# Reordering the first loads of a fused attention and token-mixing kernel: two row tiles first, the key weights in single chunks, a transpose of its own for tile 3

## The chip, the cores and the metric

One core of a Trainium2 chip runs the kernel. The metric is device time in microseconds, the median of several executions. The profile is of one more execution, and its span runs from the first to the last instruction.

## What is computed

With x of 2048 rows and 512 columns, the reference mixes two branches by a gate for each row:

```python
def _A_ref(x, wqkv, wo):                 # linear attention, 32 heads of 16
    q, k, v = split(x @ wqkv)
    phi = lambda t: where(t > 0, t + 1, exp(t)) + 1e-6
    pq, pk = phi(q), phi(k)
    kv = einsum("bhsd,bhse->bhde", pk, v)
    z = einsum("bhsd->bhd", pk)
    num = einsum("bhqd,bhde->bhqe", pq, kv)
    den = einsum("bhqd,bhd->bhq", pq, z)[..., None] + 1e-6
    return (num / den) @ wo
def _B_ref(x, w1, b1, w2, b2):           # MLP over the rows, F = 1792
    h = layernorm(x)
    u = gelu(einsum("bsd,sf->bdf", h, w1) + b1)
    return transpose(einsum("bdf,fs->bds", u, w2) + b2)
g = sigmoid((x * gate_w).sum(-1, keepdims=True))
out = g * _A_ref(x, wqkv, wo) + (1 - g) * _B_ref(x, w1, b1, w2, b2)
```

All inputs and the output are bf16.

## The kernel before

The rows are cut into 16 tiles of 128. `xs` holds x with rows on partitions, `xT` holds it with columns on partitions, in four blocks of 128 columns (k = 0 to 3). Every instruction's order on its engine is written by hand; the schedule is not planned by a tool. Each engine works through its own list and waits by semaphores, and so do the two queues from which DMAs are issued here, SP's (`nc.sync`) and ACT's (`nc.scalar`).

The stages, in order:

1. *Keys and G.* For each row tile t, four matmuls of 512 columns (`k_part`, tile `kacc`, all recorded at line 110 by the helper `mm`) multiply x's blocks by `wk_sb`, the key third of wqkv. `k_phi` then makes `pk` with an exponential on ScalarE (L216) and two operations on VectorE (L217, L220). Four tiles later `g_tile` adds x-transposed times pk into four accumulators (`gacc`). `ln_step` takes a tile's layer norm statistics on VectorE (L240, L241).
2. *The first three W1 blocks, with the queries* (`uacc`, `qacc`), from 32 us on. Their weights are the first of four chunks of W1 (`w1c`).
3. *The rest of W1*, with the small products of the attention branch in between.
4. *The output*: for each row tile, `aps` (attention) and `yps` (MLP), mixed and stored.

The transposed blocks come in two ways. Tiles 0 to 2 (`HEADS = 3`) are transposed on TensorE: `transpose_part(t, k0, k1)` multiplies blocks of `xs` by an identity into a PSUM bank `pt`, and `copy_part` copies the bank into `xT`, on ScalarE (L210) or VectorE (L212). Tiles 3 to 15 are transposed by DMA straight from the input (`load_xT`, L132), on SP's queue.

The first DMAs are issued by `load_x` (L126) and `load_wk` (L129). SP gets x0, x1 and the third chunk of Wk (Wk 2); ACT gets the first two chunks in one transfer (Wk 0-1), x2 and the fourth chunk (Wk 3). A chunk or an x tile is 128 KB. The first DMA transpose is held back: VectorE copies a few elements of x0 into the place that the transpose will write (L156), so that the transpose has to wait for that copy, and the copy for x0's landing. Behind it SP issues the transpose of tiles 5 to 7, x3, x4 to x7, and then transposes and rows in groups of four, Wq, and W1's first chunk in two halves of 1024 KB.

While the first data is on its way, TensorE runs six matmuls on constants (`warm_up(6)`, tile `wps`), and ScalarE loads its table (L196). TensorE then does tile 0's four transposes, the first two K matmuls of tile 0, the transposes of tiles 1 and 2, and the remaining ten K matmuls of the three tiles, chunk by chunk; then the loop over tiles 3 to 15 begins.

Of the kernel before, what the change touches and what calls it, by code (L numbers as in the profile page):

```python
# [15 lines left out]
def kernel(  # L16
# [13 lines left out]
    nc = tc.nc  # L30
    P = nc.NUM_PARTITIONS
# [8 lines left out]
    NT = S // P  # L40
    ND = D // P
# [15 lines left out]
    w1_view = B_w1.rearrange("(t p) f -> p t f", p=P)  # L57
# [8 lines left out]
    def keep(shape, dtype, name):  # L66
        return persist.tile(shape, dtype, name=name, tag=name)

    def bank(name, dtype=FP32):
        return ps.tile([P, SC], dtype, name=name, tag="bank")  # L70

    xs = keep([P, NT, D], BF16, "xs")
    hs = keep([P, NT, D], BF16, "hs")
    xT = keep([P, ND, S], BF16, "xT")
# [34 lines left out]
    def mm(o, lhsT, rhs, start, stop, **kw):  # L109
        nc.tensor.matmul(o, lhsT=lhsT, rhs=rhs, start=start, stop=stop, **kw)  # L110
# [14 lines left out]
    def load_x(q, t0, n):  # L125
        q.dma_start(out=xs[:, t0 : t0 + n, :], in_=x_view[:, t0 : t0 + n, :])  # L126

    def load_wk(q, k, n):
        q.dma_start(out=wk_sb[:, k : k + n, :], in_=wqkv_view[:, k : k + n, D : 2 * D])  # L129

    def load_xT(t0, n):
        nc.sync.dma_start(  # L132
            out=xT[:, :, t0 * P : (t0 + n) * P], in_=X[t0 * P : (t0 + n) * P, :], transpose=True
        )

    load_x(nc.sync, 0, 1)
    load_wk(nc.scalar, 0, 2)
    load_x(nc.sync, 1, 1)
    load_x(nc.scalar, 2, 1)
    load_wk(nc.sync, 2, 1)  # L140
    load_wk(nc.scalar, 3, 1)
    nc.vector.memset(ones_f[:], 1.0)
    nc.vector.memset(mhalf[:], -0.5)
    nc.gpsimd.memset(ident[:], 0.0)
    nc.gpsimd.affine_select(
        out=ident[:], in_=ident[:], compare_op=ALU.not_equal, fill=1.0, base=0,
# [5 lines left out]
        out=maskQ[:], in_=maskH[:].rearrange("p (a m) -> p m a", m=2), op=ALU.max, axis=AX.X  # L152
    )
    nc.gpsimd.memset(brow[:], 0.0)

    nc.vector.tensor_copy(  # L156
        out=xT[:, :, 3 * P : 3 * P + 2],
        in_=xs[:, 0, 0 : 2 * ND].rearrange("p (k c) -> p k c", k=ND),
    )
    load_xT(3, 2)  # L160
    load_xT(5, 3)
    load_x(nc.sync, 3, 1)
    load_x(nc.sync, 4, 4)
    for t0, n in ((8, 4), (12, 4)):
        load_xT(t0, n)
        load_x(nc.sync, t0, n)
# [2 lines left out]
    for c, (j0, nb) in enumerate(w1_chunks):  # L169
        w = wpool.tile([P, NT, FB * P], BF16, name="w1c", tag="wc")  # L170
        w1c.append(w)
        for t0 in range(0, NT, 8) if c == 0 else (0,):
            t1 = t0 + 8 if c == 0 else NT
            nc.sync.dma_start(
                out=w[:, t0:t1, : nb * P], in_=w1_view[:, t0:t1, j0 * P : (j0 + nb) * P]
            )
        if c == 0:
            nc.sync.dma_start(out=wv_sb[:], in_=wqkv_view[:, :, 2 * D : 3 * D])
            nc.sync.dma_start(out=wo_sb[:], in_=wo_view)
# [21 lines left out]
    def transpose_part(t, k0, k1):  # L201
        pt = pts[t, k0, k1] = bank("pt")
        for k in range(k0, k1):
            mm(pt[:, k * P : (k + 1) * P], xs[:, t, k * P : (k + 1) * P], ident[:], True, True)

    def copy_part(t, k0, k1, on_act):
        src = pts.pop((t, k0, k1))[:, k0 * P : k1 * P].rearrange("p (k s) -> p k s", k=k1 - k0)
        dst = xT[:, k0:k1, t * P : (t + 1) * P]
        if on_act:
            nc.scalar.activation(out=dst, in_=src, func=ACT.Copy)  # L210
        else:
            nc.vector.tensor_copy(out=dst, in_=src)  # L212

    def phi(dst, acc):
        e = work.tile([P, SC], BF16, name="e", tag="e", bufs=6)
        nc.scalar.activation(out=e[:], in_=acc[:], func=ACT.Exp)  # L216
        nc.vector.tensor_scalar(  # L217
            out=e[:], in0=e[:], scalar1=1.0, scalar2=PHI_EPS, op0=ALU.min, op1=ALU.add
        )
        nc.vector.scalar_tensor_tensor(  # L220
            out=dst, in0=acc[:], scalar=0.0, in1=e[:], op0=ALU.max, op1=ALU.add
        )
# [3 lines left out]
    def k_part(t, ks):  # L226
        if t not in kaccs:
            kaccs[t] = bank("kacc")
        for k in ks:
            mm(  # L230
                kaccs[t][:], xT[:, k, t * P : (t + 1) * P], wk_sb[:, k, :],
                k == 0, k == ND - 1,
            )

    def k_phi(t):
        phi(pk[:, t, :], kaccs.pop(t))
# [46 lines left out]
    def ln_step(u):  # L283
        ln_stats(u)
        if u % TPC == TPC - 1:
            ln_rstd(u // TPC)

    HEADS = 3
    for k0, k1 in ((0, 1), (1, 2), (2, ND)):
        transpose_part(0, k0, k1)  # L290
        copy_part(0, k0, k1, k0 == 2)
    k_part(0, range(2))
    for k0, k1 in ((0, 1), (1, 2), (2, ND)):
        transpose_part(1, k0, k1)
    for k0, k1 in ((0, 2), (2, ND)):
        transpose_part(2, k0, k1)
    copy_part(1, 0, 1, False)
    copy_part(1, 1, 2, True)
    copy_part(2, 0, 2, False)
    copy_part(2, 2, ND, True)  # L300
    copy_part(1, 2, ND, False)
    k_part(1, range(2))
    k_part(2, range(2))
    ln_step(0)
    for t in range(HEADS):
        k_part(t, (2,))
    for t in range(HEADS):
        k_part(t, (3,))
        k_phi(t)
    ln_step(1)  # L310
    LAG = 4
    LN_LAG = 5
# [147 lines left out]
    for j in range(NB0, NF):  # L460
        c, jj = divmod(j, FB)
# [30 lines left out]
        out=gg[:], in0=gth[:], scalar1=0.5, scalar2=0.5, op0=ALU.mult, op1=ALU.add  # L492
    )
    nc.vector.tensor_scalar(
        out=c1[:], in0=gth[:], scalar1=-0.5, scalar2=0.5, op0=ALU.mult, op1=ALU.add
# [3 lines left out]
    for t in range(NT):  # L499
        c, tl = divmod(t, TPC)  # L500
        aps = bank("aps")
        for j in range(ND):
# [3 lines left out]
            out=a_sc[:], in_=aps[:], func=ACT.Identity,  # L506
            scale=gg[:, t : t + 1], bias=c2[:, t : t + 1],
        )
        for c0, W in ((0, 2 * P), (2 * P, P), (3 * P, P)) if t == NT - 1 else ((0, D),):
            cs = slice(c0, c0 + W)  # L510
            yps = bank("yps")
            for f in range(NF):
# [6 lines left out]
                out=ot[:, :W], in0=yps[:, :W], scalar=c1[:, t : t + 1], in1=a_sc[:, cs],  # L519
# [35 lines left out]
```

## Time and profile before

| What | Before |
|---|---|
| Median of 3 runs | 162.54 us (162.47 to 163.53) |
| Profiled execution, first to last instruction (the only time that its page gives) | 160.8 us |
| TensorE busy | 156.3 us (97%) |
| VectorE busy | 124.8 us (78%) |
| ScalarE busy | 72.8 us (45%) |
| GpSimd busy | 7.3 us (5%) |
| Granted TensorE clock, mean | 1.000 |
| HBM read, written | 19.01 MB, 2.10 MB |

A line of the timeline or of a group names the engine (PE is TensorE, PEld its weight loads, DVE VectorE, ACT ScalarE, POOL GpSimd, SPq SP's queue), the source line, the operation, the tile written and the tiles read, and how many instructions were merged. A bracket gives the idle time ahead and what ended it. Matmuls are pipelined and their ends are modelled, so groups of matmuls overlap in the timeline by a little; it is the distance of their starts that says how fast they go.

### The profile page before, as it was taken

How to read it: one execution, taken by the hardware profiler on the slowest of the kernel's cores; microseconds unless marked ns; L12 is line 12 of the kernel's file. 1: busy time of each engine (PE TensorE's matmuls, PEld its weight loads, DVE VectorE, ACT ScalarE, POOL GpSimd, SP SyncE). 2: the span in 40 equal slices, each digit the busy share in tenths (PEclk: the TensorE clock that was granted, in tenths of full speed). 3: DMA queues.
4: the chain of work that ended last, by engine and by line, in shares of the span. 5: the costliest groups of instructions: out<-in, count | busy, mean ns of one | idle time of the engine just before them, and what ended most of it. 6: DMA issues, size and time to landing. Idle time of an engine off the chain costs nothing.

```text
span 160.8 us, 2241 instructions
## 1 busy us (share of the span) xinstructions
PE 156.3 (97%) x826; PEld 72.6 (45%) x840; DVE 124.8 (78%) x276; ACT 72.8 (45%) x114; POOL 7.3 (5%) x17
## 2 busy tenths in 40 slices
PE   7999999999999999999999999999999999999993
PEld 2444444444444444444444444444444444444462
DVE  1599999769999998756999999676999999711122
ACT  3552476654978483059873330237433442111110
POOL 3000332002020000000000000000000000000000
PEclk9999999999999999999999999999999999999999
DMA  5999999999970007600930689501000001110001
GB/s 165 229 235 238 274 335 295 359 348 348 335 177 0 0 0 236 225 0 5 335 120 2 186 270 288 169 33 37 33 33 33 33 33 60 47 60 33 33 33 33
DMA packets 29369, 22.94 MB, mean 143 GB/s; under 512 B 7824, under 2 KB 29328, under 8 KB 29360
## 3 DMA queue, kind: packets, MB, share of 16 engines
q1 hardware_dynamic: 28400, 21.89, 46.1%
q10 hardware_dynamic: 848, 0.79, 1.4%
q0 software_dynamic: 112, 0.14, 0.7%
q8 instruction: 6, 0.10, 0.3%
q14 instruction: 3, 0.02, 0.0%
HBM read 19.01 MB, written 2.10 MB: 131 GB/s over the span
## 4 chain that ended last, share of the span: by engine, by line
PE 94%; DVE 3%; issue 1%; ACT 0%
PE uacc L110 30%; PE yps L110 30%; PE aps L110 9%; PE qacc L110 8%; PE gacc L110 8%; PE kacc L110 7%; PE wps L110 2%; DVE pk L220 1%; DVE e L217 1%; DVE stats L240 0%; ACT e L216 0%; PE kvps L110 0%; PE pt L110 0%; PE w2ps L110 0%; DVE ot L518 0%
## 5 line engine op out<-in xcount | busy, mean ns | idle before, releaser
L110 PE MATMUL uacc<-hs,w1c 128*128 128x512 bf16 (+1 forms) x230 | 51.2, 379 | 0.3 <-issue 0.2
L110 PE MATMUL yps<-uT,w2c 128*128 128x512 bf16 (+2 forms) x247 | 50.8, 355 | 0.3
L110 PEld LDWEIGHTS <-w2c 128*128 128x128 bf16 x252 | 23.6, 98 | 25.2
L110 PEld LDWEIGHTS <-w1c 128*128 128x128 bf16 (+1 forms) x233 | 21.8, 98 | 26.0 <-issue 0.2
L505 ACT ACTIVATE a_sc<-aps,c,gg 128x512 f32<-128x512 f32 x16 | 12.4, 774 | 31.2 <-PE aps L110 15.5
L518 DVE SCALAR_TENSOR_TENSOR ot<-yps,c,a_sc 128x512 bf16<-128x512 f32 (+2 forms) x18 | 12.3, 688 | 15.4 <-PE yps L110 11.7
L339 ACT ACTIVATE uT<-uacc,bcol 128x512 bf16<-128x512 f32 x14 | 9.3, 686 | 17.5 <-PE uacc L110 17.4
L110 PE MATMUL aps<-W2sb,pqT 128*128 128x512 bf16 x63 | 16.4, 379 | 0.1
L110 PE MATMUL qacc<-xT,wq_sb 128*128 128x512 bf16 x61 | 16.1, 379 | 0.2
L110 PE MATMUL kacc<-wk_sb,xT 128*128 128x512 bf16 x63 | 15.9, 380 | 0.2
L404 DVE STREAM_TRANSPOSE zT<-pz 128x512 f32<-128x512 f32 x16 | 11.3, 705 | 6.0 <-ACT pz L403 6.0
L110 PE MATMUL gacc<-pk,xs 128*128 128x512 bf16 x63 | 15.6, 379 | 0.0
L256 ACT ACTIVATE hs<-xs,nmr,rstd 128x512 bf16<-128x512 bf16 x16 | 12.8, 805 | 2.3 <-DVE nmr L250 2.3
L403 ACT ACTIVATE pz<-pqT,zcol 128x512 f32<-128x512 bf16 x16 | 11.4, 714 | 4.8 <-DVE ot L518 4.7
L216 ACT ACTIVATE e<-kacc 128x512 bf16<-128x512 f32 x16 | 9.2, 596 | 9.7 <-PE kacc L110 9.6
L216 ACT ACTIVATE e<-qacc 128x512 bf16<-128x512 f32 x16 | 9.5, 594 | 7.7 <-PE qacc L110 7.7
L413 DVE STREAM_TRANSPOSE rex<-rd 128x512 bf16<-128x512 bf16 x16 | 11.4, 712 | 0.6
L220 DVE SCALAR_TENSOR_TENSOR pk<-kacc,e 128x512 bf16<-128x512 f32 x16 | 11.1, 692 | 0.6
L220 DVE SCALAR_TENSOR_TENSOR pqT<-qacc,e 128x512 bf16<-128x512 f32 x16 | 11.1, 691 | 0.6
L406 DVE TENSOR_REDUCE den<-zT 128x32 f32<-128x512 f32 x16 | 11.0, 686 | 0.6
L110 PEld LDWEIGHTS <-xs 128*128 128x128 bf16 x76 | 7.2, 100 | 8.3 <-DMA xs<-in_A_x_dram 0.6
L240 DVE BATCH_NORM_STATS2 stats<-xs 128x6 f32<-128x512 bf16 x16 | 10.9, 683 | 0.0
(59 smaller groups left out, 99.3 us busy)
## 6 DMA issues: line engine op xcount, KB each, us to landing
w2c<-in_B_w_dram SPq DMA_DIRECT2D x8, 896.0 KB, 5.8
w1c<-in_B_w_dram SPq DMA_DIRECT2D x2, 2048.0 KB, 15.7
w1c<-in_B_w_dram SPq DMA_DIRECT2D x3, 1024.0 KB, 9.7
out_dram<-ot SPq DMA_DIRECT2D x13, 128.0 KB, 1.7
xs<-in_A_x_dram SPq DMA_DIRECT2D x3, 512.0 KB, 4.5
wq_sb<-in_A_wqkv_dram SPq DMA_DIRECT2D x1, 512.0 KB, 6.6
wv_sb<-in_A_wqkv_dram SPq DMA_DIRECT2D x1, 512.0 KB, 10.4
wo_sb<-in_A_wo_dram SPq DMA_DIRECT2D x1, 512.0 KB, 9.1
```

The lines of the kernel that those rows point to most:

```text
L110: nc.tensor.matmul(o, lhsT=lhsT, rhs=rhs, start=start, stop=stop, **kw)
L216: nc.scalar.activation(out=e[:], in_=acc[:], func=ACT.Exp)
L220: nc.vector.scalar_tensor_tensor(out=dst, in0=acc[:], scalar=0.0, in1=e[:], op0=ALU.max, op1=ALU.add)
L240: nc.vector.bn_stats(out=stats[:], in_=xs[:, t, :])
L256: nc.scalar.activation(out=hs[:, t, :], in_=xs[:, t, :], func=ACT.Identity, scale=rstd[:, t : t + 1], bias=nmr[:, t : t + 1],)
L339: nc.scalar.activation(out=uT[:, j, :], in_=acc[:], func=ACT.Gelu_apprx_tanh, bias=bcol[:, j : j + 1])
L403: nc.scalar.activation(out=pz[:], in_=seg, func=ACT.Copy, scale=zcol[:, j : j + 1])
L404: nc.vector.transpose(out=zT[:], in_=pz[:])
L406: nc.vector.tensor_reduce(out=den[:], in_=zT[:].rearrange("p (a d) -> p a d", d=HEAD), op=ALU.add, axis=AX.X)
L413: nc.vector.transpose(out=rex[:].rearrange("p (a d) -> p a d", d=HEAD), in_=rd[:].unsqueeze(2).to_broadcast([P, SC // HEAD, HEAD]),)
L505: nc.scalar.activation(out=a_sc[:], in_=aps[:], func=ACT.Identity, scale=gg[:, t : t + 1], bias=c2[:, t : t + 1],)
L518: nc.vector.scalar_tensor_tensor(out=ot[:, :W], in0=yps[:, :W], scalar=c1[:, t : t + 1], in1=a_sc[:, cs], op0=ALU.mult, op1=ALU.add,)
```

## The change

The head of the kernel is reordered in four places. The loads: x0 leads SP's queue and x1 leads ACT's; Wk follows in four single chunks, alternating between the queues; x2 comes behind them on SP. The DMA transposes: tile 3 gets one of its own, issued directly behind x2, with no copy that holds it back; the next two take two tiles each (4 and 5, 6 and 7), and x3 to x7 come in one transfer. W1's first chunk is loaded in one DMA. And the order on the engines: tiles 0 and 1 are both transposed first, then come their first two K matmuls, then tile 2's transposes, then the other K matmuls tile by tile, and tile 0's layer norm statistics behind tile 2's phi.

```diff
     load_x(nc.sync, 0, 1)
-    load_wk(nc.scalar, 0, 2)
-    load_x(nc.sync, 1, 1)
-    load_x(nc.scalar, 2, 1)
+    load_x(nc.scalar, 1, 1)
+    load_wk(nc.sync, 0, 1)
+    load_wk(nc.scalar, 1, 1)
     load_wk(nc.sync, 2, 1)
     load_wk(nc.scalar, 3, 1)
+    load_x(nc.sync, 2, 1)
+    load_xT(3, 1)
...
-    nc.vector.tensor_copy(
-        out=xT[:, :, 3 * P : 3 * P + 2],
-        in_=xs[:, 0, 0 : 2 * ND].rearrange("p (k c) -> p k c", k=ND),
-    )
-    load_xT(3, 2)
-    load_xT(5, 3)
-    load_x(nc.sync, 3, 1)
-    load_x(nc.sync, 4, 4)
+    load_xT(4, 2)
+    load_xT(6, 2)
+    load_x(nc.sync, 3, 5)
...
-        for t0 in range(0, NT, 8) if c == 0 else (0,):
-            t1 = t0 + 8 if c == 0 else NT
-            nc.sync.dma_start(
-                out=w[:, t0:t1, : nb * P], in_=w1_view[:, t0:t1, j0 * P : (j0 + nb) * P]
-            )
+        nc.sync.dma_start(out=w[:, :, : nb * P], in_=w1_view[:, :, j0 * P : (j0 + nb) * P])
...
     HEADS = 3
     for k0, k1 in ((0, 1), (1, 2), (2, ND)):
         transpose_part(0, k0, k1)
-        copy_part(0, k0, k1, k0 == 2)
+    for k0, k1 in ((0, 2), (2, ND)):
+        transpose_part(1, k0, k1)
+    copy_part(0, 0, 1, False)
+    copy_part(0, 1, 2, True)
+    copy_part(0, 2, ND, False)
+    copy_part(1, 0, 2, True)
+    copy_part(1, 2, ND, False)
     k_part(0, range(2))
-    for k0, k1 in ((0, 1), (1, 2), (2, ND)):
-        transpose_part(1, k0, k1)
+    k_part(1, range(2))
     for k0, k1 in ((0, 2), (2, ND)):
         transpose_part(2, k0, k1)
-    copy_part(1, 0, 1, False)
-    copy_part(1, 1, 2, True)
     copy_part(2, 0, 2, False)
     copy_part(2, 2, ND, True)
-    copy_part(1, 2, ND, False)
-    k_part(1, range(2))
-    k_part(2, range(2))
+    for t in range(HEADS - 1):
+        k_part(t, (2, 3))
+        k_phi(t)
+    k_part(2, range(ND))
+    k_phi(2)
     ln_step(0)
-    for t in range(HEADS):
-        k_part(t, (2,))
-    for t in range(HEADS):
-        k_part(t, (3,))
-        k_phi(t)
     ln_step(1)
```

## The prediction

> **What bounds the kernel now.** I read the chain that ended last first, then TensorE's timeline over the first 14 us, then the DMA issues with their times to landing, and last the DMA rate by stretches. The change touches nothing but the first DMAs and the order of the first three row tiles.
>
> ```profile
> PE 94%; DVE 3%; issue 1%; ACT 0%
> ```
>
> TensorE is 94% of the chain, and over the whole run its only wait (apart from the start, 0.8 us) is 0.2 us near 65 us. So everything behind the head runs matmul behind matmul, and an edit to the head is worth exactly the shift of the moment from which TensorE runs without a gap. TensorE's timeline shows that moment:
>
> ```profile
> 0.84 2.72 PE L110 MATMUL wps<-const-bfloat16-1.0 128*128 128x512 bf16 x6 [0.84 <-PEq L539]
> 3.36 0.63 PE L110 MATMUL pt<-ident,xs 128*128 128x128 bf16 x4
> 4.06 0.62 PE L110 MATMUL kacc<-wk_sb,xT 128*128 128x512 bf16 x2
> 4.52 0.62 PE L110 MATMUL pt<-ident,xs 128*128 128x128 bf16 x8
> 5.13 4.06 PE L110 MATMUL kacc<-wk_sb,xT 128*128 128x512 bf16 x18
> 9.02 1.03 PE L110 MATMUL gacc<-pk,xs 128*128 128x512 bf16 x4
> ```
>
> Columns are start, length, then the group. One matmul's end is modelled as 0.379 us after its start, so 18 in 4.06 us are (4.06 - 0.38) / 17 = 0.2165 us a step; eight transposes in 0.62 us are (0.62 - 0.22) / 7 = 0.057 us a step. The first four transposes step at (0.63 - 0.31) / 3 = 0.107 us and the warm-up at (2.72 - 0.63) / 5 = 0.42 us: half speed, until about 4.1 us. Ten K matmuls of tiles 0 to 2 open the run at 5.13, so tile 3's first K matmul starts at 5.13 + 10 x 0.2165 = 7.30 us. That is the mark to watch. Ahead of it lie three small holes of 0.1 to 0.3 us (3.79 to 4.06, one step at 4.3, 4.98 to 5.13), under half a microsecond in all.
>
> The DMA issues, one window each, give KB and us from issue to landing, here for x0, x2, Wk 2, Wk 3 and the transposes of tiles 3-4 and 5-7:
>
> ```profile
> xs<-in_A_x_dram SPq DMA_DIRECT2D x1, 128.0 KB, 2.4
> ...
> xs<-in_A_x_dram ACTq DMA_DIRECT2D x1, 128.0 KB, 3.4
> ...
> wk_sb<-in_A_wqkv_dram SPq DMA_DIRECT2D x1, 128.0 KB, 3.4
> ...
> wk_sb<-in_A_wqkv_dram ACTq DMA_DIRECT2D x1, 128.0 KB, 4.2
> ...
> xT<-in_A_x_dram SPq DMA_TRANSPOSE x1, 3.8
> ...
> xT<-in_A_x_dram SPq DMA_TRANSPOSE x1, 3.9
> ```
>
> With the issue times of the timeline (0.81, 1.30, 1.74, 1.82, 3.45, 4.84) they landed at 3.2, 4.7, 5.15, 6.0, 7.25 and 8.7. The same rows give x1 1.27 + 3.0 = 4.3 and Wk 0-1 0.80 + 3.1 = 3.9. The rate by stretches (last two columns: DMA share, GB/s):
>
> ```profile
> 1.80:2.30 0.50, 0.50 (x3) 0.15 (x2) 0.16 (x1) 0.00 (x0) 0.39 (x2) 1.00 0.54 106
> 2.30:2.90 0.60, 0.60 (x2) 0.15 (x1) 0.00 (x0) 0.60 (x1) 0.00 (x0) 1.00 0.93 316
> 2.90:3.50 0.60, 0.60 (x4) 0.23 (x3) 0.17 (x1) 0.60 (x1) 0.00 (x0) 1.00 1.09 382
> 3.50:4.10 0.60, 0.53 (x6) 0.27 (x4) 0.39 (x2) 0.36 (x3) 0.00 (x0) 1.00 1.12 364
> 4.10:4.90 0.80, 0.80 (x9) 0.62 (x10) 0.22 (x2) 0.38 (x2) 0.00 (x0) 1.00 0.83 287
> 4.90:5.50 0.60, 0.60 (x7) 0.20 (x4) 0.60 (x3) 0.54 (x2) 0.00 (x0) 1.00 0.95 166
> ```
>
> Length times rate over the first five rows is 0.053 + 0.190 + 0.229 + 0.218 + 0.230 = 0.92 MB: exactly the seven 128 KB pieces of the head (0.917 MB). So in whatever order they go, the last of them has moved at about 4.9 us, and only then do the transposes' bytes flow.
>
> **The change, part by part.**
>
> *Order on the rings.* Before: x0, Wk 0-1, x1, x2, Wk 2, Wk 3. After: x0 and x1 side by side, Wk 0 and 1, Wk 2 and 3, x2 last, on SP. Three plain issues on ACT before and after, all done ahead of the table load at 2.30: nothing. SP gets a fourth plain issue (about 0.44 us each), done at about 2.6.
>
> *TensorE's order.* Twelve transposes and twelve K matmuls stand ahead of tile 3 before and after; only their order and waits change. Followed after: x0 at 3.2 as before, its transposes from 3.36. x1 has half the bytes of Wk 0-1, which landed at 3.9 on the same ring, so about 3.4; its transposes follow without a hole and end near 4.2. Wk 0 takes x1's old second place on SP: 4.3 (the other bound is 3.9). ACT's copies of tile 0 (0.28 us) and tile 1 (0.38 us) end at 4.1 and 4.6, ahead of use. Four K matmuls from 4.35: done at 4.35 + 4 x 0.2165 = 5.2. Now TensorE stands before x2's transposes, and queued behind them are Wk 2 and Wk 3's eight K matmuls, though their data is there. x2's landing is bounded by 5.15 (Wk 2, sixth of seven) and 6.0 (Wk 3, the last). I take 5.35: Wk 3 rode on ACT's ring beside the transposes, while x2, like Wk 2, is on SP ahead of them; the 0.2 us more are for being last. First transpose at 5.40 (x1 before: landed 4.3, weights loaded at 4.36), four of them 0.23, eight K matmuls 1.73: tile 3's mark at 7.36, against 7.30. **+0.06 us.**
>
> If no wait were left at all, the mark is 4.2 + 4 x 0.2165 + 0.23 + 1.73 = 7.0: the gain cannot pass 0.3 us. At the upper bound of x2 it is 6.05 + 0.23 + 1.73 = 8.0: +0.7 us.
>
> *Tile 3's own transpose, not held back.* The removed DVE copy (0.17 us) delayed SP's first transpose to 3.45; now it is issued at about 2.65. But its bytes queue behind x2 on SP's ring, so they still start at 4.9. Tiles 3-4 (0.26 MB) took until about 6.4 to move and 0.85 more to land; half of that moves by about 5.7, landing 6.5, at worst 7.25. Needed at 7.36: nothing. The next (tiles 4-5) waits on SP for x1's landing, over by then, and is issued before 4.9; its bytes follow: 7.6, at worst 8.7 as tiles 5-7 before. Needed at 7.36 + 0.87 = 8.23: cover 0.6 us, at worst -0.5. Queued behind on SP are tiles 6-7, x3 to x7 and tile 8: the same bytes as before, issued no later, and tile 8's transpose landed at 7.79 + 5.7 = 13.5 for a use at 15.2.
>
> The Trainium skill (DMA: Bandwidth & Descriptors, section Queues, rings and completion order) says that a completion count is written only after all earlier writes of that DMA engine, across its queues. It speaks against an early transpose: Wk 3, beside the transposes, landed 0.85 us after Wk 2, which agrees. By the rule an overtaking transpose would hold Wk 3 until tile 3's 6.5 us, and the mark would go to about 8.1.
>
> The same page (Rules for kernel authors) asks for large DMAs and so speaks against cutting Wk 0-1 in two. The stretches at 364 to 382 GB/s were made of 128 and 256 KB transfers, so the row prices the cut at nothing; the page alone would make it a loss of unknown size.
>
> *Row statistics of tile 0* (0.87 us on DVE) filled a hole at 5.74; now they stand behind phi of tile 2. DVE's run of phi starts when tile 0's K ends: 5.63 + 0.43 + 0.2 + ACT's 0.6 = 6.9 instead of 7.69, so it is 0.8 us earlier and 0.87 longer. The first G matmul needs pk of tile 0 at 7.9, and comes at 9.1. Nothing; without that cover (0.3 us before, 1.2 now) it would be its own wait.
>
> *W1's first chunk in one DMA* (2048 KB). The halves, issued at 17.04 and 19.71, landed at 26.1 and 29.1 by the medians of 9.1 and 9.4; the whole now lands about 29.4, and its first use is at 32.3. Nothing, covered by 2.9 us.
>
> **Sum.** +0.06 us on a span of 160.8 us. The page gives that execution's time only as its span; the median of the runs, 162.54 us, is 1.7 us more, which I take as unchanged: 162.6 us.
>
> **The rivals.**
> - *x2 is early* (at or before 5.2, as Wk 2 was): the mark is 7.0, time 162.54 - 0.3 = 162.2 us. For it: between 1.7 and 2.3 us only SP's queue moves bytes, so it has a start on ACT's. Against: the seven pieces share one rate, and x2 is last in line.
> - *The unheld transpose disturbs the last plain transfers*; slower. It decides as soon as x2 or Wk 3 lands later than 5.35; at Wk 3's old 6.0 the mark is 8.0, time 163.25 us. For it: Wk 3's late landing before. Against: then Wk 3 and the transposes were on different rings, while x2 now stands ahead of them on the same one. To pass 1% (1.6 us, about what a measurement of this kernel can tell from no change), x2 would have to land at about 7.
> - *A wait for tile 4's transpose takes the place of x2's*: three transposes instead of two, and tile 4 lands at 8.7. The price is 0.5 us, time 163.05 us.
> - *The release does not do what it says*: tile 3's bytes start at 4.9 all the same. I expect this; it belongs to the forecast.
>
> **How the numbers follow.** Forecast 0.60 (162.3 to 162.9), x2 early 0.15, disturbance 0.17, tile 4 late 0.08. The range of 162.1 to 163.4 takes in all four at their worked prices and leaves the far tail of the disturbance and the scatter of the runs (162.47 to 163.53) out. Faster by over 1% is past the 0.3 us that is there to gain: 0.02. Slower by over 1% is the tail of the disturbance: 0.05.
>
> **What would show it.** After: eight transposes from 3.36, four K matmuls from about 4.35, a hole of 0.2 us, four transposes at 5.4, and an unbroken K run from 5.6 whose ninth matmul is at 7.36. A mark at 7.0 means x2 was early; near 8, with x2's landing near 6, the disturbance; a hole just after the twelfth, tile 4. I am wrong altogether if TensorE has new holes beyond 10 us, or W1 is waited for at 32.

## The result and the profile after

In the comparison of 20 runs each, the changed kernel took 163.55 us (162.88 to 164.03) and the kernel before 163.16 us (162.45 to 163.62). The ratio is 1.0032, with an interval of 1.0019 to 1.0045: the change costs 0.3 to 0.7 us (0.4 between the medians, 0.5 by the ratio). The profiled execution of the changed kernel has a span of 161.7 us, against 160.8.

TensorE's timeline of the changed kernel, over the stretch that was shown of before:

```profile
0.84 2.72 PE L110 MATMUL wps<-const-bfloat16-1.0 128*128 128x512 bf16 x6 [0.84 <-PEq L532]
3.49 1.03 PE L110 MATMUL pt<-ident,xs 128*128 128x128 bf16 x8
4.39 1.09 PE L110 MATMUL kacc<-wk_sb,xT 128*128 128x512 bf16 x4
6.24 0.40 PE L110 MATMUL pt<-ident,xs 128*128 128x128 bf16 x4 [0.75 <-DMA xs<-in_A_x_dram]
6.47 3.62 PE L110 MATMUL kacc<-wk_sb,xT 128*128 128x512 bf16 x16
9.93 1.03 PE L110 MATMUL gacc<-pk,xs 128*128 128x512 bf16 x4
```

The order is the predicted one; one time is not. The fourth transposed group, x2's, starts at 6.24 and not at 5.40, and its bracket names the DMA of `xs`. The K run of 16 opens at 6.47, so tile 3's first K matmul, the mark of the prediction, starts at 6.47 + 8 x 0.2165 = 8.20 us, against 7.30. Those 0.90 us are the whole difference of the two spans.

The same wait stands at the head of the chain that ended last (start, length, what), where it takes 4 us from x2's issue on:

```profile
2.19 4.00 DMA xs<-in_A_x_dram
6.19 0.05 issue
6.24 0.40 PE pt L110 x4
6.63 3.45 PE kacc L110 x16
```

The DMA issues of the changed kernel, KB and us from issue to landing, for x0, Wk 2, Wk 3 and x2:

```profile
xs<-in_A_x_dram SPq DMA_DIRECT2D x1, 128.0 KB, 2.6
...
wk_sb<-in_A_wqkv_dram SPq DMA_DIRECT2D x1, 128.0 KB, 3.8
wk_sb<-in_A_wqkv_dram ACTq DMA_DIRECT2D x1, 128.0 KB, 4.3
xs<-in_A_x_dram SPq DMA_DIRECT2D x1, 128.0 KB, 4.0
```

Issued at 0.81, 1.73, 1.74 and 2.19, they land at 3.45, 5.55, 6.0 and 6.2. Before, with the same bytes, the last landing was Wk 3's at 6.0, and only the tenth K matmul of the run used it; now the last landing is x2, and tile 2's transposes and eight K matmuls stand behind it.

### The profile page after: what moved, and what is told of

The parts are those of the page before. It is cut to its first block, busy times and chain, and to the rows that moved or that the text cites. A ratio compares the mean times of both kernels' runs of the same rounds, so it can differ in the third digit from the quotient of the medians.

```text
span 161.7 us, 2252 instructions
## 1 busy us (share of the span) xinstructions
PE 157.3 (97%) x840; PEld 72.7 (45%) x840; DVE 124.7 (77%) x274; ACT 73.0 (45%) x114; POOL 7.3 (4%) x17
## 4 chain that ended last, share of the span: by engine, by line
PE 94%; DMA 2%; SPq 1%; DVE 0%; issue 0%
PE uacc L110 30%; PE yps L110 30%; PE qacc L110 9%; PE gacc L110 9%; PE aps L110 9%; PE kacc L110 8%; DMA xs<-in_A_x_dram 2%; SPq L129 1%; PE kvps L110 0%; SPq L126 0%; PE pt L110 0%; PE w2ps L110 0%; DVE ot L511 0%; PE pt L338 0%
```

## The experiments

Two questions were open: which part of the change costs, and why x2 lands at 6.2 us and not at 5.35. Each kernel has one profiled execution and its timed runs; a ratio is to the kernel before, timed beside it on the same chip; an interval is given behind each. The loads of x and Wk in the head are called plain transfers, to tell them from the DMA transposes. Besides the lines of the profile I give, read from the trace, landings of the single parts of a transfer and the start of its last 1 KB piece. A transfer's landing is counted in 16 steps, and the profile counts 16 DMA engines to a core; I take one step for the part of one engine, though the trace does not name the engine.

### Three more profiles of the same two kernels

> The kernel before, unchanged, for a second profile of its head. If the first profile was typical, tile 3's first K matmul starts at 7.2 to 7.4 us again. The 20 runs of before spread from 162.45 to 163.62 us, though, and that profile's span of 160.8 us belongs to their lower end; if the head's DMA landings are what spreads them, this profile can show a mark up to 8 us, with Wk 2 or Wk 3 landing later than 5.15 and 6.0.

Measured: a span of 160.9 us, the G run from 9.14, so the mark is 9.14 - 8 x 0.2165 = 7.41. Typical of the first profile, as far as it went.

> The kernel before, unchanged, a third profile. Two of them have a span of 160.8 and 160.9 us, while its timed runs spread over 1.1 us. If the moment at which TensorE leaves half speed is what spreads them (4.1 us in the first profile, about 5.8 in the run with before's loads and the new order), this profile shows either a mark near 7.3 again, or, in a slow run, K matmuls of 0.43 us a step after 5 us and a mark of up to 8.2.

Measured: a span of 162.0 us, 1.2 us more than the first profile of the very same kernel. TensorE's timeline in this third profile of before:

```profile
3.49 0.61 PE L110 MATMUL pt<-ident,xs 128*128 128x128 bf16 x4
4.20 1.01 PE L110 MATMUL kacc<-wk_sb,xT 128*128 128x512 bf16 x2
5.01 1.06 PE L110 MATMUL pt<-ident,xs 128*128 128x128 bf16 x8
```

Eight transposes take 1.06 us here and took 0.62 in the first profile, and two K matmuls 1.01 instead of 0.62: TensorE is still at half speed. The steps fall from 0.427 to 0.216 us only at 6.8 us (before: 4.1), and the mark is at 8.47. The loads are not what delays it (x2 lands at 4.9 against 4.7, Wk 3 at 5.8 against 6.0).

> The changed kernel unchanged, for a second profile. If the first was typical, x2 lands at 6.0 to 6.3 again and tile 3's mark is at 8.0 to 8.3; x0 lands at 3.4 to 3.6, later than before's 3.2, since ACT's first transfer is smaller and starts to share the rate sooner.

Measured: a span of 162.2 us, half speed until 6.6 us, x2 at 6.67, mark 8.68.

The five profiles side by side:

| Kernel | Full speed from | x2 lands | Wk 3 lands | Mark | Span | Span less mark |
|---|---|---|---|---|---|---|
| before | 4.1 | 4.7 | 6.0 | 7.30 | 160.8 | 153.5 |
| before, second | 3.5 | 4.8 | 5.5 | 7.41 | 160.9 | 153.5 |
| before, third | 6.8 | 4.9 | 5.8 | 8.47 | 162.0 | 153.5 |
| changed | 4.4 | 6.2 | 6.0 | 8.20 | 161.7 | 153.5 |
| changed, second | 6.6 | 6.7 | 6.5 | 8.68 | 162.2 | 153.5 |

The last column is the same in all five: what follows the mark does not differ. The moment of full speed spreads the kernel before over 1.2 us, about what its timed runs spread (162.45 to 163.62). The two profiles of the changed kernel differ by 0.5 us only: in the second, x2's wait is shorter (0.50 us against 0.75), since the four K matmuls ahead of it take 1.91 us at half speed instead of 1.09. In these profiles, then, the change costs 0.9 us where full speed comes early and 0.2 where it comes late. Two profiles do not give the spread of a kernel: the changed kernel's 20 timed runs reach from 162.88 to 164.03, about as far as before's.

The Trainium skill (TensorE: Matmul & The Clock Gate, section What's actually happening) describes this: the clock opens after a busy window of some 3.4 us that runs freely and does not start with the kernel. The profiles agree: with TensorE at work from 0.84 or 0.85 us on in all of them, full speed came between 3.5 and 6.8 us, a spread of 3.3 us. In a run with long holes (below) the clock's changes lie 6.83 and 3.41 us apart, two such windows and one. The page puts the variation from run to run at only 500 ns up or down; the profiles here show more, and they decide.

### Is it the wait for x2?

```diff
-            mm(pt[:, k * P : (k + 1) * P], xs[:, t, k * P : (k + 1) * P], ident[:], True, True)
+            mm(pt[:, k * P : (k + 1) * P], xs[:, min(t, 1), k * P : (k + 1) * P], ident[:], True, True)
```

> The changed kernel, but tile 2's transposes on TensorE read x1 in place of x2 (tile 2's keys are then those of tile 1): the wait for x2 is taken away and nothing else. Theory place: the transposes start at 5.35 without a hole, the K matmuls wait for Wk 2 (5.55) and Wk 3 (near 6.0); tile 3's mark near 7.6 instead of 8.2, ratio 1.000 to 1.001. If the ratio stays near 1.003, the wait for x2 is not what costs.

Measured: ratio 1.0005 (0.9985 to 1.0024). In its timeline the transposes follow the K matmuls without a bracket:

```profile
4.54 1.66 PE L110 MATMUL kacc<-wk_sb,xT 128*128 128x512 bf16 x4
6.03 0.39 PE L110 MATMUL pt<-ident,xs 128*128 128x128 bf16 x4
6.26 3.62 PE L110 MATMUL kacc<-wk_sb,xT 128*128 128x512 bf16 x16
```

x2 landed at 6.65 here, after all these transposes. Waiting for it would have put the mark at 6.70 + 0.23 + 1.73 = 8.66; it is at 6.26 + 8 x 0.2165 = 7.99. That is still later than the 7.6 expected, for two reasons that this trace does not separate: full speed came at 5.8 us (four K matmuls in 1.66 us), and Wk 2, the next operand in line, landed only at 6.21. The time goes back to that of before. The intervals of this ratio and the change's overlap a little; the two ratios differ by 0.0027, and an interval for the difference, worked out from the two, is 0.0004 to 0.0050. So the wait for x2 is what costs; all the rest of the edit is still in this kernel and costs nothing that can be told.

### Is it the new order on the engines?

Here the loads, the hold and the transposes stay as before; only the part from `HEADS = 3` to `ln_step(1)` is that of the changed kernel.

> The loads, the hold and the transposes of before, with only the new order of the first three tiles on TensorE, ScalarE and VectorE. Theory loads (the new line of loads is what costs; one DMA engine falls 0.6 us behind from Wk 2 on, and x2 stands last): x2 still lands at 4.7, its transposes wait little, the eight K matmuls wait for Wk 3 at most until 5.5 to 6.0; tile 3's mark at 7.1 to 7.5, ratio 0.998 to 1.001. Theory order (the new order itself loses time by its chain of copies): mark above 7.8, ratio 1.003 or more.

Measured: ratio 1.0002 (0.9982 to 1.0021), x2 at 4.76, Wk 3 at 5.79. Full speed came at 5.8 us, so this profile's mark is late, at 8.14: four K matmuls take 1.50 us, against 1.09 in the changed kernel's first profile. The timed runs show no cost: the order alone costs nothing that can be told, and neither do the layer norm statistics behind tile 2's phi.

### Does it help to use x2 later, or to load it earlier?

First the loads of the changed kernel with another order of use: after the first K matmuls of tiles 0 and 1,

```diff
-    for k0, k1 in ((0, 2), (2, ND)):
-        transpose_part(2, k0, k1)
-    copy_part(2, 0, 2, False)
-    copy_part(2, 2, ND, True)
     for t in range(HEADS - 1):
         k_part(t, (2, 3))
-        k_phi(t)
+    for k0, k1 in ((0, 2), (2, ND)):
+        transpose_part(2, k0, k1)
+    copy_part(2, 0, 2, False)
+    copy_part(2, 2, ND, True)
+    k_part(HEADS, range(ND))
     k_part(2, range(ND))
-    k_phi(2)
+    for t in (0, 1, HEADS, 2):
+        k_phi(t)
...
-    for t in range(HEADS, NT):
+    for t in range(HEADS + 1, NT):
```

> The changed kernel's loads, with another order on TensorE: Wk 2 and 3 are used for tiles 0 and 1 first, then come x2's transposes, tile 3's K matmuls, and only then tile 2's. Theory place (x2 lands near 6.2, and what costs is that eight K matmuls stand behind it): TensorE works from Wk 2's landing near 5.5 on; the first G matmul starts near 9.5 instead of 9.93 (9.02 in the profile of before), ratio to before 1.000 to 1.002. If the whole line of loads is late, Wk 3 (6.0) holds TensorE as x2 did, and the ratio stays at 1.003.

Measured: ratio 1.0022 (1.0005 to 1.0039), first G matmul at 9.73. x2 landed at 6.45 and was waited for by nobody, but Wk 2 and Wk 3, now the first to be used, landed at 5.9 and 6.2. Full speed came at 5.9. A part at most is won back, and 1.0022 and the change's 1.0032 can't be told apart: the whole end of the line is late, not x2 alone.

Then the loads, with x2 and Wk 2 exchanged on SP's queue:

```diff
-    load_wk(nc.sync, 2, 1)
-    load_wk(nc.scalar, 3, 1)
-    load_x(nc.sync, 2, 1)
+    load_x(nc.sync, 2, 1)
+    load_wk(nc.scalar, 3, 1)
+    load_wk(nc.sync, 2, 1)
```

> The changed kernel with x2 and Wk 2 exchanged on SP's queue: x2 third, Wk 2 last. Theory place (what is last in line lands near 6.2 whatever it is): x2 lands near 5.5 or earlier, Wk 2 near 6.2; tile 2's transposes are then done early, but the eight K matmuls start with Wk 2, so only the transposes' 0.23 us are gained: mark 8.0, ratio 1.002. If the lateness belongs to x2 itself and not to the last place, Wk 2 lands by 5.6 and the mark goes to 7.5, ratio 1.000.

Measured: ratio 1.0012 (0.9992 to 1.0032). x2 lands at 5.3, Wk 2, now last, at 5.84; TensorE's timeline shows two short waits in place of x2's long one:

```profile
4.19 1.04 PE L110 MATMUL kacc<-wk_sb,xT 128*128 128x512 bf16 x4
5.34 0.40 PE L110 MATMUL pt<-ident,xs 128*128 128x128 bf16 x4
5.88 3.61 PE L110 MATMUL kacc<-wk_sb,xT 128*128 128x512 bf16 x16
```

The mark is 7.61. Wk 2's landing lies between the 6.2 and the 5.6 of the two theories, the mark is nearer to the second (full speed came early here, at 3.8), and the ratio agrees with both. The last in line is later than the 5.15 of before's Wk 2, but not by as much as x2 was; with x2 third, its transposes, at least, are done by then.

### Is it the unheld transpose?

The copy that held the first transpose is put back, ahead of `load_xT(3, 1)`:

```diff
+    nc.vector.tensor_copy(
+        out=xT[:, :, 3 * P : 3 * P + 2],
+        in_=xs[:, 0, 0 : 2 * ND].rearrange("p (k c) -> p k c", k=ND),
+    )
```

> The changed kernel with the copy that holds tile 3's transpose back until x0 has landed. Theory release (the transpose issued at 2.67 overtakes x2 and slows the last plain transfers): x2 lands near 5.4 instead of 6.2, TensorE's hole before x2's transposes shrinks from 0.75 us to about 0.2, ratio to before 1.000 to 1.001. Theory place (x2 is last in line, and eight K matmuls stand behind it, so whatever delays the last transfer is paid in full): the transposes' bytes start at 4.5 to 4.9 in any case, x2 still lands near 6, ratio 1.003 as for the changed kernel.

Measured: ratio 1.0039 (1.0025 to 1.0054), x2 at 6.27, mark 8.28. The hold wins nothing that can be told.

Then the same copy on GpSimd, reading x2 instead of x0:

> The changed kernel with tile 3's transpose held back until x2 itself has landed (by a copy on the otherwise idle GpSimd). Nothing transposes while plain transfers are under way. Both theories: x2 lands at 5.2 to 5.5, undisturbed. If x2 still lands near 6, the transposes do not delay it at all, and its place at the end of the line alone does. The price: tile 3's transpose is issued 3 us later, starts near 6.5 and lands near 7.7 or later, so a new hole of 0.3 to 1 us before tile 3; ratio 1.002 to 1.007.

Measured: ratio 1.022 (1.018 to 1.026). The first byte of a transpose moves at 7.7 us, and still x2 takes 3.8 us to land, at 6.0:

```profile
xs<-in_A_x_dram SPq DMA_DIRECT2D x1, 128.0 KB, 3.8
```

The line is late without any transpose. The single parts say a little more. With the transpose held, 15 of x2's 16 parts were in by 5.67 us (5.56 in the run held by x2), and one alone came at 6.27 (6.03). With the transpose released, 14 of the 16 came together, from 6.00 to 6.19, and in the changed kernel's second profile all 16, from 6.50 to 6.67. So the release changes how the parts come in. Whether it also adds a few tenths to the last of them, four profiles can't settle; the timed runs (1.0039 held by x0, 1.0032 released) show no gain from holding. The price of holding them is far above what was expected, since not one but two of them are then waited for (engine, whom it waited for, us in total, times, longest):

```profile
PE kacc L110 <- DMA xT<-in_A_x_dram: 2.2, 2, 1.3
```

Here TensorE also fell back to half speed at 11.8 us, behind these holes, until 15.2 us.

Last, the release alone, in the kernel before (its copy taken out):

> The kernel before without the copy that holds its first transpose back (tiles 3 and 4, then issued near 2.2 us): one part of the change alone. Theory release: Wk 2 and Wk 3 land 0.5 us or more later than 5.15 and 6.0, Wk 3's three K matmuls wait, ratio 1.002 to 1.005. Theory place: Wk 3 is used only by the tenth K matmul, so a late landing is mostly covered, ratio 0.999 to 1.001.

Measured: ratio 0.9992 (0.9974 to 1.0009), Wk 3 at 5.5, the transposes of tiles 3 and 4 at 6.6 instead of 7.2, mark 7.27. The release alone is harmless, as theory place had it, and useless: 7.2 was already ahead of the mark.

### Is it the cut of Wk, or one more transfer?

The cut alone, in the kernel before:

```diff
-    load_wk(nc.scalar, 0, 2)
+    load_wk(nc.scalar, 0, 1)
+    load_wk(nc.scalar, 1, 1)
```

> The kernel before with Wk 0-1 cut into two 128 KB transfers on ACT's queue: the cut alone. Theory pieces: one DMA engine straggles by 0.5 us at Wk 3 or Wk 2, part of it covered since Wk 3 is used by the tenth K matmul, ratio 1.000 to 1.003. Theory side by side: landings within 0.2 us of before's, ratio 1.000.

Measured: ratio 1.0066 (1.0034 to 1.0099). That is no less than the whole change costs; the intervals overlap, and two of the ten runs (165.8 us) lift the ratio (the medians, 163.90 and 163.12, differ by 0.5%). Theory pieces had the cause, and the price too low. x2 lands at 6.07 instead of 4.7, though it stands in its old place, and TensorE waits for it. The eight transposes of tiles 1 and 2, in one piece in each of the three profiles of before, fall apart:

```profile
4.94 0.39 PE L110 MATMUL pt<-ident,xs 128*128 128x128 bf16 x4
6.12 0.40 PE L110 MATMUL pt<-ident,xs 128*128 128x128 bf16 x4 [0.79 <-DMA xs<-in_A_x_dram]
```

Of Wk 2's 16 parts, 12 landed by 4.87 and four between 5.53 and 5.89; the same four-part lag shows in x2 and Wk 3. A few DMA engines are some 0.6 us behind the others, and a transfer has landed only when the last of them is done. A lag of this kind is not new with the seventh transfer: in the first profile of before, ten parts of Wk 3 landed by 5.35 and six between 5.63 and 6.03. There it is smaller and stays in the last transfer, which is used late.

The reverse, in the changed kernel: Wk 0-1 in one transfer on ACT's queue again.

> The changed kernel with Wk 0 and Wk 1 again as one 256 KB transfer on ACT's queue (six plain transfers instead of seven; x0 and x1 still lead, x2 still last on SP, now third there). Theory pieces (cutting Wk and a fourth transfer on SP's queue make one DMA engine fall behind): all engines land x2 within 0.3 us of each other, x2 by 5.5, mark near 7.6, ratio 1.001. Theory side by side (x0 beside x1 makes it): the straggling engine stays, x2 at 6.0 to 6.3, ratio 1.003.

Measured: ratio 1.0043 (1.0015 to 1.007). x2 lands at 5.63 and the bytes end at 5.1, so the lag is smaller (13 parts of x2 by 5.23, three between 5.52 and 5.63). But the pair, now behind x1 on its queue, lands at 4.84 instead of Wk 0's 4.35 and Wk 1's 4.63, and the first K matmul starts at 4.88: the mark is 7.70. This profile is better than the changed kernel's, but it is of the fastest execution of the ten (163.11 us); the timed runs are no better, and they do not settle what the repair is worth.

The other pair, Wk 2 and 3 in one transfer, with Wk 0 and 1 left cut:

> The changed kernel with Wk 2 and Wk 3 in one 256 KB transfer on ACT's queue, behind x1 and Wk 1; Wk 0 and 1 stay cut; six plain transfers, x2 third and last on SP. Theory count (a seventh transfer makes engines fall behind): the bytes end at 4.9 to 5.1, x2 lands by 5.4, Wk 2-3 by 5.6, mark 7.2 to 7.5, ratio 0.998 to 1.001. Theory cut (the single chunks of Wk side by side make them fall behind): the bytes end after 5.5, x2 or Wk 2-3 land near 6, ratio 1.002 to 1.004.

Measured: ratio 1.0040 (1.0025 to 1.0055). x2, third on SP, lands at 5.32, but the pair lands at 6.04 and eight K matmuls stand behind it; the bytes end at 5.6. These are the numbers of theory cut and not of theory count: six transfers were late too. That Wk 0 and 1 are still cut need not be the reason, as the next run shows.

A seventh transfer with hardly any bytes, in the kernel before:

```diff
     load_wk(nc.scalar, 0, 2)
+    extra = keep([P, 16], BF16, "extra")
+    nc.scalar.dma_start(out=extra[:], in_=x_view[:, 15, 0:16])
```

> The kernel before with one more transfer on ACT's queue behind Wk 0-1: 128 rows of 32 bytes (4 KB) into a tile that nothing reads. Seven transfers with hardly more bytes. Theory count: the last plain bytes move at 5.3 or later instead of 4.9 to 5.1, Wk 3 lands near 6, ratio 1.002 to 1.006 as in the run with Wk 0-1 cut. Theory cut: the bytes end at 5.0 to 5.2, ratio 1.000 to 1.002.

Measured: ratio 1.0037 (1.0022 to 1.0053). Four kilobytes, and no cut of Wk, cost as much as the whole change, as theory count had it (the bytes end at 5.8, Wk 3 lands at 6.15). The DMA issues of this kernel:

```profile
wk_sb<-in_A_wqkv_dram SPq DMA_DIRECT2D x1, 128.0 KB, 4.0
xs<-in_A_x_dram ACTq DMA_DIRECT2D x1, 128.0 KB, 4.1
wk_sb<-in_A_wqkv_dram ACTq DMA_DIRECT2D x1, 128.0 KB, 3.8
extra<-in_A_x_dram ACTq DMA_DIRECT2D x1, 4.0 KB, 3.2
```

Wk 2, whose issue did not move, lands at 5.71 instead of 5.15: 15 of its parts by 4.77, the last one 0.94 us later. x2 lands at 5.88, and TensorE waits 0.8 us for it, as in the changed kernel:

```profile
PE pt L110 <- DMA xs<-in_A_x_dram: 0.8, 1, 0.8
```

Finally a head with fewer transfers: from the kernel before without the hold, x2 leaves the head, tile 2 is transposed by a DMA of its own behind Wk 2, and tile 0's K is finished before tile 1's.

```diff
-    load_x(nc.scalar, 2, 1)
...
-    load_xT(3, 2)
-    load_xT(5, 3)
-    load_x(nc.sync, 3, 1)
+    load_xT(2, 1)
+    load_xT(3, 2)
+    load_xT(5, 3)
+    load_x(nc.sync, 2, 2)
...
-    HEADS = 3
+    HEADS = 2
...
+    for k0, k1 in ((0, 2), (2, ND)):
+        transpose_part(1, k0, k1)
+    copy_part(1, 0, 2, False)
+    copy_part(1, 2, ND, True)
+    k_part(0, (2, 3))
+    k_part(1, range(ND))
```

> From the kernel before: x2 leaves the head (tile 2 is transposed by a DMA of its own, released, behind Wk 2), so five plain transfers are left; tile 0's K is finished while tile 1's copies run. Theory count: no engine falls behind, the plain bytes end near 4.5, Wk 3 lands by 5.0; tile 0's and 1's K end near 6.0, tile 2's transpose lands by 6.2, tile 3's mark at 6.9 to 7.3 instead of 7.3 to 7.4, ratio 0.997 to 0.9995. If transposes land later (tile 2 after 6.5), ratio 1.000 or more.

Measured: ratio 0.9993 (0.9977 to 1.0008). The plain bytes end at 4.5, Wk 2 lands last, at 5.1, tile 2's transpose at 6.1. Full speed came at 5.5 us and the mark is 7.57, so this profile can't show the gain of the loads. The timing can't tell this kernel from the one before.

> The same with the 4 KB transfer behind Wk 0-1 on ACT's queue, six transfers in all. Theory count (the seventh is one too many): landings as in the run with five, 0.1 to 0.2 us later, ratio within 0.001 of it. Theory small transfer (a short transfer between long ones makes an engine fall behind, whatever the number): one or more engines land Wk 2 and Wk 3 0.5 us or more after the others, ratio higher by 0.002 to 0.004.

Measured: ratio 1.0015 (1.0000 to 1.0030), 0.0022 above the run with five, though the two intervals overlap. Fourteen parts of Wk 2 landed by 4.80, two at 5.34 and 5.37, and the bytes end at 5.15. Theory small transfer had this, and a count of seven is no threshold: an extra transfer makes engines lag here too.

The end of the plain bytes, by the start of the last 1 KB piece, in all profiles:

| Transfers in the head | Last piece starts |
|---|---|
| five | 4.5 |
| five and the 4 KB one | 5.15 |
| six, arranged as before (five profiles) | 4.9 to 5.1 |
| six, Wk 0-1 whole behind x1 | 5.1 |
| six, Wk 2-3 whole | 5.6 |
| seven (nine profiles) | 5.3 to 6.2 |

In the changed kernel half of the bytes have moved at 3.50 us, before at 3.47: the loss comes in the second half.

## Why the prediction was wrong

- *The forecast* of +0.06 us was too low by 0.3 to 0.5 us: the measured change is +0.4 us between the medians, +0.5 by the ratio. It is also off in its base, by more: before's 162.54 us was a median of three, and over 20 runs it is 163.16. Both are needed for the measured 163.55 us to lie 0.15 above the range.
- *The step that failed* is the choice of x2's landing between 5.15 and 6.0. The 5.35 measured as 6.2 and 6.7 in the two profiles. In the first, those 0.85 us are the whole miss of the mark (8.20 against 7.36). The rest of that chain held: 6.2 gives a mark of 8.2 where the prediction's own upper bound, worked from 6.0, gave 8.0.
- *Why the bound was read wrong.* "In whatever order they go, the last of them has moved at about 4.9 us" took the sum of bytes for the end of the work. The sum held for half of the bytes and not for the rest: in the changed kernel the last piece starts only at 5.68. With Wk 0-1 cut, or with the 4 KB transfer more, single parts lag by 0.5 to 0.9 us, and a landing waits for the last of 16. I had priced the cut at nothing from the rate of the stretches, an average over engines that can't show one straggler. The parts of before's own Wk 3 showed one (six of them 0.3 to 0.7 us behind the tenth), and its other two profiles have that landing at 5.5 and 5.8; the reason given for it, that Wk 3 rode beside the transposes, is not borne out, since it landed at 5.5 where the transposes were released earlier. The prediction had the Trainium skill's rule on large transfers (DMA: Bandwidth & Descriptors, Rules for kernel authors) beside it and let the row win. In the kernel before the runs took the side of the rule: the cut alone measured 1.0066 (1.0034 to 1.0099), although what they show is lagging engines and not a lower rate. In the changed kernel, making either pair of chunks one transfer again won nothing (1.0043 and 1.0040).
- *The rival of the disturbed transfers* had the time nearly right (mark 8.0, 163.25 us), but its cause is not borne out: holding the transpose back won nothing, and x2 was late even where no transpose moved before 7.7 us. What the prediction worked out from the rule on completion counts, Wk 3 held until tile 3's transpose lands, did not happen either: Wk 3 landed at 6.0 and 6.5 in the two profiles, the transpose at 6.8 and 7.2.
- *x2 early* did not happen. *Tile 4's transpose* was no wait: tiles 4 and 5 landed at 7.9, needed at 9.1; tile 3's at 6.8, needed at 8.2.
- *Smaller terms.* x0 landed at 3.45 and not at 3.2, and the first transposes started at 3.49, +0.13. ACT's first transfer now starts to move at 1.97 instead of 2.33 us and shares the rate sooner, but that this is the reason is not shown: in before's second and third profiles x0 landed at 3.48 and 3.45 as well. x1 landed at 3.6 (3.4 foreseen), Wk 0 at 4.35 (4.3).
- *What was right:* the path (x2's transposes with eight K matmuls queued behind), that the mark sets the whole time, that no more than 0.3 us could be gained (nothing was), the layer norm statistics, and W1's first chunk, issued at 17.84 and landed 11.9 us later at 29.7, for a use at 33.2.
- *The base.* "The moment from which TensorE runs without a gap" was taken from one profile. It was one of those in which full speed comes early; in the third the mark of the same kernel is 1.2 us later, and against it the changed kernel's second profile is only 0.2 us later still.

What stays open is why a further transfer makes single DMA engines lag. That it does is shown by the 4 KB transfer and the cut; whether it is the number, the place on ACT's queue or the way in which the two queues' pieces meet is not. The traces show one thing more: in the run with six transfers and the 4 KB one, a single 1 KB piece on SP's queue took 0.74 us instead of 0.046, at 4.15 us, and one part of Wk 2 was late; in the changed kernel four pieces took 0.5 to 0.7 us, between 3.57 and 3.74. But with Wk 0-1 cut no 1 KB piece after 2.4 us took as much as 0.2 us, and four parts were late all the same, so such pieces are not the whole reason. No version beat the kernel before by more than the timing can tell: the release alone (0.9992) and the head with five transfers (0.9993) came nearest.

## What to carry to other kernels

Order loads so that the transfer that lands last is used last: here a last landing at 6.0 us cost nothing as the operand of the tenth K matmul, and one at 6.2 cost 0.9 us ahead of four transposes and eight K matmuls. TensorE, which takes its list in order here, pays a late operand with everything queued behind it, so ask of each wait what stands behind it and not only how long it is. A sum of bytes over a rate held here for the first half of the bytes and missed the end by 0.8 us; take the last landing from the latest one in the trace, and look whether it was covered there. And before a few tenths of a microsecond at the head are forecast from one profile, look at a second and a third.

## What the runs showed of the hardware

- Nearly the same bytes, one transfer more: 4 KB behind Wk 0-1 came with one part in 16 of Wk 2 landing 0.94 us after the other 15, and cost the kernel 0.37% (0.22 to 0.53).
- The moment at which TensorE leaves half speed lay between 3.5 and 6.8 us in the eighteen profiles; between the first and the third profile of one and the same kernel it moved the span by 1.2 us.
- Two holes, of 0.85 and 1.33 us, in one stretch of 3.41 us (8.39 to 11.80, TensorE busy for 1.43 us of it) were followed by half speed from 11.8 to 15.2 us. In the changed kernel the one hole of 0.75 us (busy for 2.67 us of the 3.42 from 4.41 on) was not.
- With a transpose issued at 2.67 us behind the last plain transfer on SP's queue, 14 to 16 parts of that transfer landed within 0.25 us of each other (five profiles); with the transpose held, 15 of the 16 came over 0.5 to 0.6 us and the last 0.5 to 0.6 us behind them (two profiles).
